# Memory-query products of the key/value gradients: from four 32-row products to one full product with a block diagonal operand

## The chip, the cores and the metric

The kernel runs on one core of a Trainium2 chip. The core has five engines with instruction streams of their own: TensorE (PE; its weight loads are listed as PEld), VectorE (DVE), ScalarE (ACT), GpSimd (POOL) and SyncE (SP), which in this kernel issues most of the DMA transfers. Sixteen DMA engines move the data between the chip's memory and the on-chip memory of 128 partitions. The metric is the device time of one execution in microseconds (us); lower is better.

## The reference

Forward and backward pass of a gated mix of two attention branches over 2048 tokens of width 576. Branch A has 32 query heads of width 18 and one shared key/value head. Branch B cuts the sequence into 64 segments of 32 tokens and carries 8 memory tokens from segment to segment; it has 32 heads of width 128. Cut to what matters:

```python
for s in range(n_seg):                       # 64 segments, in order
    h = concat([mem, x[s]])                  # 8 memory tokens, then 32 tokens
    q, k, v = h @ Wq, h @ Wk, h @ Wv         # 32 heads x 128
    p = softmax(mask(q @ k.T * scale))       # memory rows see the memory, tokens see memory and the past
    o = (p @ v) @ Wo
    mem = o[:8]                              # memory of the next segment
    outs.append(o[8:])
out = g * A(x) + (1 - g) * concat(outs)      # g = sigmoid(x . gate_w)
grads = vjp(grad_out)                        # x, all weights, mem0, gate_w
```

In the gradient, the key gradient of a token is the sum over the queries that saw it, `dk = dS^T q`, and its value gradient is `dv = P^T dO`. The queries are of two sorts: the tokens of the same segment, and the 8 memory rows of the segment. The change concerns the second sort. For 128 tokens (a tile of four segments) there are 4 x 8 = 32 memory queries per head.

## The kernel before

All of branch B's backward pass after the scores is in three stages, and the change touches the second and third of them, and a detail of the forward pass.

**Forward chain** (`b_chain_fwd`, woven with `a_pass1`): 64 segments in order. In each, the memory rows' attention ends with value products, 16 small matrix products into the tile `c_x`: eight with the weights `t2["v"]` on `PBm` (64 columns per region `u`), then eight with `vx` on `PBx` (32 columns), which add to them. `PBm` and `PBx` come from GpSimd (`expand`, line 264), one behind the other.

**Backward chain** (`b_chain_bwd`, woven with `a_pass2`): the segments in reverse order. Each segment is a list of 16 pieces (the `yield`s); after each piece the weaving emits one step of `a_pass2`, the backward pass of branch A: two products `b_S`, two `b_dP`, eight small ones into `b_acc`, one exponential on ScalarE (`b_E`) and two products on VectorE (`b_dS`). `a_pass2` loads `b_QS` from SP for every four steps; the load is emitted five steps before its first use and has three buffers.

From the fifth segment on, the pieces also carry key/value gradients of tokens that the chain has already passed: `kv_load`, `kv_mm` and `kv_out`, numbered by `n`. `n // 2` names a block of four heads `g` of a token tile `tt`; even `n` is the value gradient, odd `n` the key gradient. There are 4 x 8 x 11 / 2 = 176 of them (11 of the 16 token tiles), four per segment, in 44 segments. `kv_mm(n)` fills one bank of PSUM, the tile `r_x` of 128 tokens x 4 heads x 128:

- for each of the four heads, the memory queries: weights `kvS` (32 memory queries x 128 tokens, probabilities or score gradients), moving operand `kvR` (32 memory queries x 128, the rows of dO or of q), at the 32 partitions `rg` of the array;
- for each head, the tokens: weights `r_ks` (128 x 128), moving operand `r_kr` (128 x 128), which add to the same place.

`kv_mm(n)` ends with `kv_load(n + 2)`. For even `n` that is one load of `kvS` and two of `kvR` (dO from `mtok["dO"]`, q from `row_dram["q"]`), then `r_ks` and `r_kr`. `kvS` and `kvR` are one tile each, of which consecutive blocks use the four groups of 32 partitions in turn. All of these loads, those of the chain itself (`load_a`, `load_b`, `load_c`, `load_dT`) and those of `b_QS` stand in SP's one instruction stream, in the order in which the pieces emit them. In the built program each load from SP also waits for the eighth load before it to land.

**Behind the chain** (`b_post`): the remaining 6 token tiles, eight steps of four heads each, 48 steps. `st_KV` computes key and value gradients as above (tiles `y_pk`; operands `y_sB`, `y_mR` for the memory queries), `st_T` transposes them, `st_H` multiplies by the weights into `y_pdx`. `load_s` loads the memory queries of a whole token tile (twelve loads) a token tile ahead; `load` brings `y_ds`, `y_q`, `y_p`, `y_dO` and the transposed `y_dq` for every two steps.

Who writes the memory operands: `pq_dram` comes from GpSimd (`x_rows`, line 1009), with the memory index of the token tile in the order head-of-four `i`, memory row `q`, segment `s`; a segment's columns outside its own 32 tokens are zero.

Of the kernel before, what the change touches and what calls it, by code (L numbers as in the profile page):

```python
# [16 lines left out]
P = 128  # L17
# [5 lines left out]
E = 128  # L23
# [23 lines left out]
class Kern:  # L47
# [41 lines left out]
    def setup_consts(self, pool):  # L89
        nc = self.nc  # L90
        self.identB = pool.tile([P, P], BF16, name="identB")
        nc.gpsimd.memset(self.identB[:], 0.0)
        nc.gpsimd.affine_select(out=self.identB[:], in_=self.identB[:], compare_op=ALU.not_equal,
                                fill=1.0, base=0, pattern=[[-1, P]], channel_multiplier=1)
        self.identF = pool.tile([P, P], F32, name="identF")
        nc.vector.tensor_copy(self.identF[:], self.identB[:])

# [168 lines left out]

    def mem_rows(self, tt, c, cs):
        dO = self.mtok["dO"][tt * 32:(tt + 1) * 32, 1024 * c + cs.start:1024 * c + cs.stop]
        return (dO.rearrange("(s q) e -> q s e", s=4),
                self.row_dram["q"][4 * tt:4 * tt + 4, 32 * c:32 * c + 8, cs].rearrange("s q e -> q s e"))  # L270

# [57 lines left out]
    def b_chain_fwd(self, keep, sp, psum):  # L329
# [69 lines left out]
        for s in range(NSEG):  # L399
# [550 lines left out]
    def b_chain_bwd(self, wot, sp, kd, kvp, keep, psum):  # L950
# [7 lines left out]
        pads = {w: keep.tile([P, 8, 32], BF16, name=f"r_{w}pad") for w in ("p", "ds")}  # L958
        kvS = kvp.tile([P, 4, 2, P], BF16, name="r_kvS")
        kvR = kvp.tile([P, 2, 4, E], BF16, name="r_kvR")  # L960
        dT = kd.tile([P, 3, HB, 32], BF16, name="r_dT")
# [53 lines left out]
        def kv_at(n):  # L1015
            v, w = n // 2, n % 2
            return slice(32 * (v % 4), 32 * (v % 4) + 32), w, self.NTT - 1 - v // 8, v % 8

        def kv_load(n):
            if n >= NKV:  # L1020
                return
            rg, w, tt, g = kv_at(n)
            if w == 0:
                nc.sync.dma_start(kvS[rg].rearrange("p i x k -> p i (x k)"),
                                  self.pq_dram[tt, g // 2].rearrange("i q s h x k -> (q s) i h (x k)")[:, :, g % 2, :])
                for j, src in enumerate(self.mem_rows(tt, g // 2, slice(512 * (g % 2), 512 * (g % 2) + 512))):
                    nc.sync.dma_start(kvR[rg, j].rearrange("p i e -> p (i e)"), src)
            a = kvp.tile([P, 4, P], BF16, name="r_ks", bufs=3)
            nc.sync.dma_start(a[:], (self.dsx_dram if w else self.px_dram)[tt][:, 4 * g:4 * g + 4, :])
            b = kvp.tile([P, 4, P], BF16, name="r_kr", bufs=3)  # L1030
            nc.sync.dma_start(b[:].rearrange("p h e -> p (h e)"),
                              self.xtok["q" if w else "dO"][tt * P:(tt + 1) * P, 512 * g:512 * g + 512])
            kvl[n] = (a, b)

        def kv_mm(n):
            if not 0 <= n < NKV:
                return
            rg, w, tt, g = kv_at(n)
            a, b = kvl.pop(n)
            pk = psum.tile([P, 4, P], F32, name="r_x", bufs=1)  # L1040
            for i in range(4):
                self.mm(pk[:, i, :], lhsT=kvS[rg, i, w, :], rhs=kvR[rg, w, i, :], start=True, stop=False, tp=(rg.start, 0))
            for i in range(4):
                self.mm(pk[:, i, :], lhsT=a[:, i, :], rhs=b[:, i, :], start=False, stop=True)
            kvo[n] = pk
            kv_load(n + 2)

        def kv_out(n):
            if not 0 <= n < NKV:
                return  # L1050
            rg, w, tt, g = kv_at(n)
# [174 lines left out]
    def b_post(self, sp, rp, wH, psum):  # L1226
# [5 lines left out]
        NC = NG // 2  # L1232
        pdx, C, sB, mR, T_ = {}, {}, {}, {}, {}

        def load_s(n):
            tt = NTT - 1 - n
            if tt >= 0:
                sB[tt] = sp.tile([P, 4, 2, 2, P], BF16, name="y_sB", bufs=2)
                mR[tt] = sp.tile([P, 2, 8, E], BF16, name="y_mR", bufs=2)
                for c in range(4):  # L1240
                    r = slice(32 * c, 32 * c + 32)
                    nc.sync.dma_start(sB[tt][r].rearrange("p i h x k -> p i (h x k)"),
                                      self.pq_dram[tt, c].rearrange("i q s h x k -> (q s) i (h x k)"))
                    for j, src in enumerate(self.mem_rows(tt, c, slice(0, 1024))):
                        nc.sync.dma_start(mR[tt][r, j].rearrange("p u e -> p (u e)"), src)

# [15 lines left out]
        def st_KV(t):  # L1262
            tt, g, r, d = NTT - 1 - t // 8, t % 8, slice(4 * (t % 2), 4 * (t % 2) + 4), C[t // 2]
            pks = {w: psum.tile([P, 4, P], F32, name="y_pk", bufs=2) for w in ("dk", "dv")}
            c, h2 = slice(32 * (g // 2), 32 * (g // 2) + 32), g % 2
# [47 lines left out]
        load_s(0)  # L1313
        load(1, ("ds", "q", "p", "dO"))
        load(0, ("dq",))
        load(2, ("ds", "q", "p", "dO"))
        load(1, ("dq",))
        load(2, ("dq",))
        load_s(1)
# [837 lines left out]
```

## Time and profile before

| | |
|---|---|
| median of three runs | 5495.77 us (5483.73 to 5498.1) |
| profiled execution, from its first to its last instruction | 5509.8 us |
| mean granted clock of TensorE | 0.983 |
| DMA traffic | 1012.49 MB in 1107113 packets |

The profiled execution's own span is 14 us above the median; the profile gives no other time of it. Busy times of TensorE in the stages (windows of the profile):

| stretch, us | what runs | PE busy, us | DMA share |
|---|---|---|---|
| 420 to 2130 | forward chain with `a_pass1` | 1643.62 of 1710 | 0.62 |
| 2130 to 2815 | tokens' attention (`b_bulk`) | 612.16 of 685 | 0.81 |
| 2815 to 2954 | backward chain, before the first key/value gradient | 112.02 of 139 | 0.65 |
| 2954 to 4096 | backward chain with key/value gradients | 1096.18 of 1142 | 0.92 |
| 4096 to 4490 | backward chain, rest | 352.94 of 394 | 0.68 |
| 4490 to 4731 | `b_post` | 230.99 of 241 | 0.92 |
| 4731 to 5510 | weight gradients, last products | 757.31 of 779 | 0.66 |

How to read the lines that are shown below: a line of a tile names the line of the kernel, the engine, the operation, the tile written and the tiles read, how many there are, and the duration in ns (shortest/median/longest). Matrix products are all recorded at line 82, a helper, so they are told apart by their tiles. A timeline's line begins with its start and its duration in us; in square brackets stands how long the engine had been idle before it, and what released it. A matrix product's duration contains the way through the array, so the pace of products is read from the starts. "SPq" are the transfers that SP issues: the duration there is that of issuing, and is not counted as busy time of an engine; the DMA share is the mean busy share of the sixteen DMA engines.

### The profile page before, as it was taken

The page shows a single profiled execution, that of the slowest core. Times are in us where ns is not written, and L with a number is a line of the kernel's source. Part 1 is how long each engine was busy: PE and PEld are TensorE (multiplying, and loading weights), DVE is VectorE, ACT ScalarE, POOL GpSimd, SP SyncE. Part 2 cuts the span into 40 slices and gives each one's busy share as a digit, 9 for nine tenths or more (in the row PEclk, how much of TensorE's full clock was granted, in tenths as well). Part 3 has the DMA queues.
Part 4 walks back from the last instruction along what each step waited for, and adds up shares of the span by engine and source line. Part 5 has one row for each costly group of instructions (what it writes and reads, how often), then busy time and mean ns, then how long its engine had stood idle before and what let it go on. Part 6 is the DMA issues. An engine that isn't in the chain of part 4 may idle for free. (4 is left out here: it accounts for less than half of the span.)

```text
span 5509.8 us, 204884 instructions
## 1 busy us (share of the span) xinstructions
PE 5191.1 (94%) x87077; PEld 2903.4 (53%) x87077; DVE 3717.0 (67%) x6812; ACT 3494.6 (63%) x5264; POOL 2300.6 (42%) x4322
## 2 busy tenths in 40 slices
PE   7999999999999998999979999999998989999999
PEld 6434444444444445777744555555554457764444
DVE  5337888788888887888868888888888851121112
ACT  4327878788878886888858887778777752111101
POOL 4004555555555545555534444444444421122213
PEclk9999999999999998999989999999999999999999
DMA  6646666666665545888885899999987679976653
GB/s 215 229 173 135 136 136 135 134 137 140 138 133 121 117 108 163 256 253 261 253 257 153 206 216 205 201 206 211 204 189 145 141 167 274 262 222 228 208 161 122
DMA packets 1107113, 1012.49 MB, mean 184 GB/s; under 512 B 666674, under 2 KB 919355, under 8 KB 1096594
## 3 DMA queue, kind: packets, MB, share of 16 engines
q1 hardware_dynamic: 1002642, 752.11, 57.2%
q0 software_dynamic: 100016, 242.38, 14.3%
q8 instruction: 681, 11.16, 0.9%
q10 hardware_dynamic: 3536, 4.90, 0.3%
q14 instruction: 238, 1.95, 0.1%
HBM read 547.90 MB, written 383.13 MB: 169 GB/s over the span
## 5 line engine op out<-in xcount | busy, mean ns | idle before, releaser
L1736 DVE TENSOR_TENSOR a_W<-a_dP,a_E 128x512 bf16<-128x512 f32 x2048 | 1314.7, 684 | 276.2 <-issue 129.4
L1876 DVE TENSOR_TENSOR b_dS<-b_dP,b_E 128x512 bf16<-128x512 f32 x2048 | 1311.6, 684 | 245.4 <-issue 108.1
L1853 ACT ACTIVATE b_E<-b_S 128x1024 bf16<-128x1024 f32 x1024 | 1048.2, 1024 | 298.3 <-PE b_dP L82 229.8
L1706 ACT ACTIVATE a_E<-a_S 128x1024 bf16<-128x1024 f32 x1024 | 1049.9, 1025 | 261.2 <-PE a_dP L82 170.2
L82 PEld LDWEIGHTS <-b_QS 32*128 32x128 bf16 (+1 forms) x8192 | 257.5, 92 | 549.6 <-issue 481.1
L82 PE MATMUL r_pj<-WT,r_dT 128*32 128x288 bf16 x12288 | 496.0, 288 | 10.4 <-issue 10.2
L82 PE MATMUL b_S<-b_KV,b_QS 32*128 32x512 bf16 x2048 | 406.0, 387 | 97.5 <-ACT b_E L1853 62.4
L82 PE MATMUL w_acc<-w_d,w_h 128*128 128x512 bf16 (+1 forms) x2400 | 473.8, 379 | 0.0
L82 PE MATMUL a_S<-a_QD,l_KV 32*128 32x512 bf16 x2048 | 400.8, 385 | 41.8 <-ACT a_E L1706 35.3
L82 PE MATMUL b_acc<-b_dS,b_QS 128*32 128x512 bf16 x2048 | 427.8, 395 | 1.1 <-DVE b_dS L1876 0.9
L82 PE MATMUL a_acc<-a_W,l_WK 128*32 128x512 bf16 x4096 | 414.6, 391 | 0.3 <-DVE a_W L1736 0.2
L82 PE MATMUL a_acc<-a_E,l_VK 128*32 128x512 bf16 x4096 | 405.3, 381 | 10.2 <-issue 5.6
L82 PE MATMUL b_acc<-b_E,b_QS 128*32 128x512 bf16 x2048 | 410.2, 396 | 0.5 <-issue 0.5
L82 PE MATMUL b_dP<-b_KV,b_QS 32*128 32x512 bf16 x2048 | 404.7, 391 | 0.0
L82 PE MATMUL a_dP<-a_QD,l_KV 32*128 32x512 bf16 x2048 | 399.9, 387 | 0.0
L82 PEld LDWEIGHTS <-r_dT 128*32 128x32 bf16 x12288 | 333.3, 97 | 107.4 <-issue 16.8
L82 PEld LDWEIGHTS <-w_h 128*128 128x128 bf16 (+1 forms) x2688 | 229.9, 100 | 258.3 <-issue 6.6
L82 PEld LDWEIGHTS <-hm 128*32 128x32 bf16 x7680 | 204.0, 97 | 196.4 <-issue 2.6
L79 ACT CAST w_o<-w_acc 128x512 bf16<-128x512 f32 x54 | 31.6, 585 | 384.3 <-PE w_acc L82 367.9
L783 POOL TENSOR_TENSOR x_P<-x_E,x_r 128x512 bf16<-128x512 bf16 x128 | 152.7, 1193 | 293.6 <-DVE x_r L780 293.6
L77 DVE CAST w_o<-w_acc 128x512 bf16<-128x512 f32 x54 | 37.3, 691 | 335.2 <-PE w_acc L82 308.9
L82 PEld LDWEIGHTS <-l_KV 32*128 32x128 bf16 x4096 | 121.7, 91 | 254.3 <-issue 209.6
(464 smaller groups left out, 10903.3 us busy)
## 6 DMA issues: line engine op xcount, KB each, us to landing
b_QS<-qs_dram SPq DMA_DIRECT2D x256, 256.0 KB
dOx_dram<-p_tok SPq DMA_DIRECT2D x16, 1024.0 KB
c_vx<-vx_dram SPq DMA_DIRECT2D x64, 256.0 KB
krow_dram<-c_k POOLq DMA_DIRECT2D x64, 256.0 KB
qrow_dram<-c_q POOLq DMA_DIRECT2D x64, 256.0 KB
vrow_dram<-c_v POOLq DMA_DIRECT2D x64, 256.0 KB
x_q<-qx_dram SPq DMA_DIRECT2D x32, 512.0 KB
x_k<-kx_dram SPq DMA_DIRECT2D x32, 512.0 KB
```

Of the source, the lines that this page charges most:

```text
L77: nc.vector.tensor_copy(out, in_)
L79: nc.scalar.copy(out, in_)
L82: return self.nc.tensor.matmul(out, lhsT, rhs, start=start, stop=stop, tile_position=tp, skip_group_check=True)
L783: nc.gpsimd.tensor_tensor(out=o[:, r, :], in0=Et[:, :, lo:lo + n], in1=rl[:].unsqueeze(2).to_broadcast([P, 4, n]), op=ALU.mult)
L1706: nc.scalar.activation(E_[n][:], S.pop(n)[:], ACT.Exp, scale=SCALEA)
L1736: nc.vector.tensor_tensor(out=W_[n][:, i, :], in0=dP[i][:], in1=E_[n][:, i, :], op=ALU.mult)
L1853: nc.scalar.activation(E_[n][:], S.pop(n)[:], ACT.Exp, scale=SCALEA)
L1876: nc.vector.tensor_tensor(out=D_[n][:, i, :], in0=dP[i][:], in1=E_[n][:, i, :], op=ALU.mult)
```

## The change

- The memory queries of four heads become one operand. `kvS` is now a tile of 128 rows (4 heads x 32 memory queries), and `kvR` a tile of 128 rows x (dO or q) x 4 heads x 128 in which only the blocks of a row's own head are filled: a block diagonal. The other blocks are zeroed once by VectorE when the tiles are made, and never written again. One product of 128 rows and 512 columns replaces four of 32 rows and 128 columns.
- `kv_mem` makes the tiles, two pairs in the chain and four in `b_post`, and clears them. `kv_mem_load` loads one block of four heads: S in one load, R in eight, one for each head and for dO and q, each of 32 rows of 256 bytes.
- In `b_post`, `load_s` loads by step (`t + 4`), not by token tile, and `st_KV` finishes one of the two tiles before it begins the other.
- In the forward chain the two loops over `u` become one: for each region the product on `PBm` is followed by that on `PBx`.
- `identF`, a copy of the identity matrix for branch A's forward pass, is made where it is used.

In the built program, TensorE's 704 short products into `r_x` become 176 and the 384 into `y_pk` become 96; SP issues 528 loads more in the chain and 360 more in `b_post`; the order of everything else stays.

```diff
+    def kv_mem(self, pool, name, bufs):
+        S = [pool.tile([P, 2, P], BF16, name=f"{name}S{i}") for i in range(bufs)]
+        R = [pool.tile([P, 2, 4, E], BF16, name=f"{name}R{i}") for i in range(bufs)]
+        for t in R:
+            self.nc.vector.memset(t[:].rearrange("p x i e -> p (x i e)").bitcast(F32), 0.0)
+        return S, R
+
+    def kv_mem_load(self, S, R, tt, g):
+        c, h = g // 2, g % 2
+        self.nc.sync.dma_start(S[:].rearrange("p x k -> p (x k)"),
+                               self.pq_dram[tt, c].rearrange("i q s h x k -> (i q s) h (x k)")[:, h, :])
+        for i in range(4):
+            r, c0 = slice(32 * i, 32 * i + 32), 512 * h + 128 * i
+            for x, src in enumerate((
+                    self.mtok["dO"][tt * 32:(tt + 1) * 32, 1024 * c + c0:1024 * c + c0 + E].rearrange("(s q) e -> q s e", s=4),
+                    self.row_dram["q"][4 * tt:4 * tt + 4, 32 * c:32 * c + 8, c0:c0 + E].rearrange("s q e -> q s e"))):
+                self.nc.sync.dma_start(R[r, x, i, :], src)
...
                 self.mm(po[:, u, :], lhsT=t2["v"][:, u, :], rhs=PBm[:, u, :], start=True, stop=False)
-            for u in range(8):
                 self.mm(po[:, u, 0:32], lhsT=vx[:, u, :], rhs=PBx[:, u].rearrange("p c q -> p (c q)"),
...
-                nc.sync.dma_start(kvS[rg].rearrange("p i x k -> p i (x k)"),
-                                  self.pq_dram[tt, g // 2].rearrange("i q s h x k -> (q s) i h (x k)")[:, :, g % 2, :])
-                for j, src in enumerate(self.mem_rows(tt, g // 2, slice(512 * (g % 2), 512 * (g % 2) + 512))):
-                    nc.sync.dma_start(kvR[rg, j].rearrange("p i e -> p (i e)"), src)
+                self.kv_mem_load(kvS[g % 2], kvR[g % 2], tt, g)
...
-            for i in range(4):
-                self.mm(pk[:, i, :], lhsT=kvS[rg, i, w, :], rhs=kvR[rg, w, i, :], start=True, stop=False, tp=(rg.start, 0))
+            self.mm(pk[:].rearrange("p i e -> p (i e)"), lhsT=kvS[g % 2][:, w, :],
+                    rhs=kvR[g % 2][:, w].rearrange("p i e -> p (i e)"), start=True, stop=False)
...
-                for c in range(4):
-                    r = slice(32 * c, 32 * c + 32)
-                    nc.sync.dma_start(sB[tt][r].rearrange("p i h x k -> p i (h x k)"),
-                                      self.pq_dram[tt, c].rearrange("i q s h x k -> (q s) i (h x k)"))
-                    for j, src in enumerate(self.mem_rows(tt, c, slice(0, 1024))):
-                        nc.sync.dma_start(mR[tt][r, j].rearrange("p u e -> p (u e)"), src)
+        sB, mR = self.kv_mem(sp, "y_m", 4)
+
+        def load_s(t):
+            if t < NG:
+                self.kv_mem_load(sB[t % 4], mR[t % 4], NTT - 1 - t // 8, t % 8)
...
-            for x, w in ((1, "dk"), (0, "dv")):
-                for i in range(4):
-                    self.mm(pks[w][:, i, :], lhsT=sB[tt][c, i, h2, x, :], rhs=mR[tt][c, x, 4 * h2 + i, :],
-                            start=True, stop=False, tp=(c.start, 0))
-            for w, s_, r_ in (("dk", "ds", "q"), ("dv", "p", "dO")):
+            for x, w, s_, r_ in ((1, "dk", "ds", "q"), (0, "dv", "p", "dO")):
                 pk = pks[w]
+                self.mm(pk[:].rearrange("p i e -> p (i e)"), lhsT=sB[t % 4][:, x, :],
+                        rhs=mR[t % 4][:, x].rearrange("p i e -> p (i e)"), start=True, stop=False)
...
-                    if t % 8 == 7:
-                        load_s(t // 8 + 2)
+                    load_s(t + 4)
...
+        self.identF = keep.tile([P, P], F32, name="identF")
+        nc.vector.tensor_copy(self.identF[:], self.identB[:])
```

More of the change, by code (lines that the diff above doesn't have):

```diff
@@ L94, in setup_consts @@
                                 fill=1.0, base=0, pattern=[[-1, P]], channel_multiplier=1)
-        self.identF = pool.tile([P, P], F32, name="identF")
-        nc.vector.tensor_copy(self.identF[:], self.identB[:])
     XT0 = 5
@@ L265, in expand @@
                                      in1=self.bmask[:].unsqueeze(1).to_broadcast([P, n, 4, 8]), op=ALU.mult)
[L267 to L270, printed above, removed]
+    def kv_mem(self, pool, name, bufs):
[14 more added lines that the diff above has]
+                self.nc.sync.dma_start(R[r, x, i, :], src)
     def m_rows(self, t, c):
@@ L958, in b_chain_bwd @@
         pads = {w: keep.tile([P, 8, 32], BF16, name=f"r_{w}pad") for w in ("p", "ds")}
-        kvS = kvp.tile([P, 4, 2, P], BF16, name="r_kvS")
-        kvR = kvp.tile([P, 2, 4, E], BF16, name="r_kvR")
+        kvS, kvR = self.kv_mem(kvp, "r_kv", 2)
         dT = kd.tile([P, 3, HB, 32], BF16, name="r_dT")
@@ L1016, in kv_at @@
             v, w = n // 2, n % 2
-            return slice(32 * (v % 4), 32 * (v % 4) + 32), w, self.NTT - 1 - v // 8, v % 8
+            return w, self.NTT - 1 - v // 8, v % 8
         def kv_load(n):
@@ L1037, in kv_mm @@
                 return
-            rg, w, tt, g = kv_at(n)
+            w, tt, g = kv_at(n)
             a, b = kvl.pop(n)
             pk = psum.tile([P, 4, P], F32, name="r_x", bufs=1)
-            for i in range(4):
-                self.mm(pk[:, i, :], lhsT=kvS[rg, i, w, :], rhs=kvR[rg, w, i, :], start=True, stop=False, tp=(rg.start, 0))
+            self.mm(pk[:].rearrange("p i e -> p (i e)"), lhsT=kvS[g % 2][:, w, :],
+                    rhs=kvR[g % 2][:, w].rearrange("p i e -> p (i e)"), start=True, stop=False)
             for i in range(4):
@@ L1050, in kv_out @@
                 return
-            rg, w, tt, g = kv_at(n)
+            w, tt, g = kv_at(n)
             o = kvp.tile([P, 4, P], BF16, name="r_kvo", bufs=2)
@@ L1232, in b_post @@
         NC = NG // 2
[L1233 to L1239, printed above, removed]
-                for c in range(4):
-                    r = slice(32 * c, 32 * c + 32)
-                    nc.sync.dma_start(sB[tt][r].rearrange("p i h x k -> p i (h x k)"),
-                                      self.pq_dram[tt, c].rearrange("i q s h x k -> (q s) i (h x k)"))
-                    for j, src in enumerate(self.mem_rows(tt, c, slice(0, 1024))):
-                        nc.sync.dma_start(mR[tt][r, j].rearrange("p u e -> p (u e)"), src)
+        pdx, C, T_ = {}, {}, {}
+        sB, mR = self.kv_mem(sp, "y_m", 4)
+        def load_s(t):
+            if t < NG:
+                self.kv_mem_load(sB[t % 4], mR[t % 4], NTT - 1 - t // 8, t % 8)
         def load(c, names):
@@ L1314, in b_post @@
         load(1, ("ds", "q", "p", "dO"))
+        load_s(1)
         load(0, ("dq",))
         load(2, ("ds", "q", "p", "dO"))
+        load_s(2)
         load(1, ("dq",))
+        load_s(3)
         load(2, ("dq",))
-        load_s(1)
         hist = [self.hist_to_dram(a, b, sp, psum, "y_pt", 2, g)
```

3 lines of the change are left out of this document (1 added, 2 removed).

## The prediction

> **What bounds the kernel now.** I read the views in this order: the windows of the two stages in which the change works, the instructions of the tiles that it replaces, SP's timeline (SP issues these loads), and TensorE's timeline and waits beside it. The windows first; the columns are the stretch, its length, busy time (and instructions) of PE, PEld, DVE, ACT and POOL, the granted clock, the share of the DMA engines and GB/s.
>
> ```profile
> core 0: us, PE busy (x) PEld busy (x) DVE busy (x) ACT busy (x) POOL busy (x), PEclk, DMA share, GB/s
> 2954.00:4096.00 1142.00, 1096.18 (x22992) 591.54 (x22989) 956.28 (x1659) 920.96 (x1224) 550.39 (x1008) 0.99 0.92 205
> 4490.00:4731.00 241.00, 230.99 (x2488) 185.73 (x2487) 41.73 (x116) 55.95 (x105) 33.86 (x61) 0.96 0.92 247
> ```
>
> The first is the part of the backward chain that carries key/value products: 176 of them, four per segment, so 44 segments at 1142/44 = 25.95 us. The second is the stage behind the chain (`b_post`). TensorE is busy 96% of both, and nearly all its gaps are filled, so it sets the pace; but the DMA engines stand at 0.92, and nothing here shows SP, whose issues are not counted as busy. So I took the replaced tiles:
>
> ```profile
> L82 PE MATMUL r_x<-r_kvR,r_kvS x704: 211/214/309, 2954.0 to 4095.7; 32*128 32x128 bf16 x176
> L1024 SPq DMA_DIRECT2D r_kvS<-pq_dram x88: 325/424/1334, 2935.6 to 4073.9; - x88
> L1027 SPq DMA_DIRECT2D r_kvR<-dOm_dram x88: 671/692/1170, 2936.0 to 4074.3; - x88
> L1027 SPq DMA_DIRECT2D r_kvR<-qrow_dram x88: 643/644/2316, 2936.8 to 4075.1; - x88
> L82 PE MATMUL y_pk<-y_mR,y_sB x384: 214/214/309, 4499.7 to 4720.3; 32*128 32x128 bf16 x192
> L1245 SPq DMA_DIRECT2D y_mR<-dOm_dram x24: 660/661/727, 4492.8 to 4663.2; - x24
> L1245 SPq DMA_DIRECT2D y_mR<-qrow_dram x24: 643/644/709, 4493.6 to 4663.9; - x24
> ```
>
> The reader is to see the price of issuing one load of 32 memory rows: 0.64 to 0.69 us, the same whether a row's piece is 1 KB (`r_kvR`) or 2 KB (`y_mR`). It isn't the bytes that are paid for. SP issues one behind the other:
>
> ```profile
> 3515.44 0.34 SPq L1834 DMA_DIRECT2D b_QS<-qs_dram  x1
> ...
> 3519.27 0.53 SPq L1834 DMA_DIRECT2D b_QS<-qs_dram  x1
> 3519.85 0.42 SPq L1024 DMA_DIRECT2D r_kvS<-pq_dram  x1
> 3520.32 0.69 SPq L1027 DMA_DIRECT2D r_kvR<-dOm_dram  x1
> 3521.05 0.64 SPq L1027 DMA_DIRECT2D r_kvR<-qrow_dram  x1
> ```
>
> About 0.05 us lies between an issue and the next. I summed SP's rows of its timeline from 3200 to 3800 us: 665 issues in 23 segments, 475.0 us. With the gaps that is 475.0 + 665 x 0.05 = 508 us of 600, or 20.65 + 1.45 = 22.1 us of issuing in a segment of 26.1 us. SP is 85% full. And it is already late at times, at a load that has nothing to do with the memory queries:
>
> ```profile
> 3518.63 0.39 PE L82 MATMUL r_x<-WoTt,dm 128*32 128x512 bf16 x4
> 3520.38 0.39 PE L82 MATMUL b_S<-b_KV,b_QS 32*128 32x512 bf16 x2 [1.36 <-DMA b_QS<-qs_dram]
> ...
> 3524.38 0.39 PE L82 MATMUL r_x<-r_kvR,r_kvS 32*128 32x128 bf16 x4
> 3524.71 0.40 PE L82 MATMUL r_x<-r_kr,r_ks 128*128 128x128 bf16 x4
> 3525.04 0.39 PE L82 MATMUL b_S<-b_KV,b_QS 32*128 32x512 bf16 x2
> ```
>
> `b_QS` was issued at 3515.44 and used from 3520.38: landing takes some 5 us. The code issues it five steps of 1.55 us, 7.75 us, before its use, so SP may be no more than about 2.7 us behind the order of the program before TensorE waits.
>
> **The change, part by part.**
>
> *Wide products.* From 3524.38 to 3524.71 four products of 128 columns take 0.33 us. One of 512 columns goes at the pace of the weight gradients, 420.3 us for 1920, 0.22 us. Saved: 0.11 x 176 = 19 us in the chain. In `b_post` eight short ones per step (31.2 us for 384, 0.65 us) become two (0.44 us): 0.21 x 48 steps = 10 us. These 29 us count only where TensorE sets the pace; in the sum below it doesn't, so they count nothing.
>
> *Loads in the chain.* Per block of four heads there was one load of S and two of R. Now it is one of S and eight of R, each with 32 pieces of 256 B from the same pattern of rows. S keeps its bytes and its 128 pieces, and I leave it at 0.47. The trace has no such R load. The nearest rows are the two `r_kvR` lines, which differ only in the length of a piece, which didn't matter between 1 and 2 KB: I take their median, 0.66. The cheapest row with pieces of 256 B for 32 partitions (with four pieces per partition) is
>
> ```profile
> L683 SPq DMA_DIRECT2D x_kmB<-km_dram x128: 302/430/1392, 2133.0 to 2785.8; - x128
> ```
>
> whose 0.30 I keep as the lower end. Per segment (two blocks): 16 x (0.66 + 0.05) = 11.4 us come, 2 x (0.69 + 0.68 + 0.10) = 2.9 us go (means of that stretch). SP's work becomes 22.1 + 8.5 = 30.6 us in a segment that TensorE could do in 25. SP becomes the pace: 30.6 - 25.95 = 4.6 us x 44 = **+204 us**, rounded to +200.
> The other ends: SP's rows hold stalls. At their shortest durations they make 18.2 us with gaps; if the stalls vanish, 18.2 + 8.5 = 26.7, +33 us. Upwards: in the built program each load from SP waits for the eighth before it to land, and at 3535.24 an `r_kvR` load waited for an `r_k` load issued 6.3 us earlier. At 6.3/8 = 0.78 us per load, 41 loads (29 + 12) take 32 us; +6.3 x 44 = 277 us. What waits behind the R loads on SP are `r_ks`/`r_kr` of the same product, then the loads of the next segment's chain, and `b_QS`; TensorE waits for `b_QS` first, in front of `b_S`, and with it the exponentials of ScalarE and the products of VectorE.
>
> *Loads in b_post.* Each of 48 steps now issues its own 9 loads; before, 12 served eight steps. Two steps: 2 x (0.44 + 8 x 0.655) + 18 x 0.05 = 12.3 us; with four loads of `y_ds`, `y_q`, `y_p`, `y_dO` and a transposed `y_dq`, at least 1.92 + 1.32 us, 15.5 us; at their means there (2.37 + 0.20 + 1.77) 16.6 us. So 24 x 15.5 = 372 to 398 us, where TensorE needs about 216. TensorE can't run ahead: the product of step t wants its own loads. I take 385. The first R load waits for VectorE to clear the buffers, behind a copy that ends at 4496.9, while SP arrives at 4492.8: +4.5 us. Last product at 4490 + 4.5 + 385 + 2 (landing) = 4881 for 4720: **+160 us** (145 to 190; at 0.30 + 0.05 per load two steps are 9.9 us, 238 us in all, +15).
>
> *Value products in the forward chain.* Eight products on `c_PBm` stood ahead of the first on `c_PBx`; now one does. POOL's and TensorE's rows:
>
> ```profile
> 1005.45 0.63 POOL L264 TENSOR_TENSOR c_PBx<-c_pn,bmask 128x256 bf16<-128x256 bf16 x1
> ```
>
> ```profile
> 1005.95 0.41 PE L82 MATMUL c_x<-c_PBm,c_v 128*128 128x64 bf16 x8
> 1006.19 0.36 PE L82 MATMUL c_x<-c_PBx,c_vx 128*128 128x32 bf16 x8
> 1006.73 0.39 PE L82 MATMUL a_S<-a_QD,l_KV 32*128 32x512 bf16 x2 [0.18 <-ACT a_E L1706]
> ```
>
> `c_PBx` is done at 1006.08; the second product would now be ready at 1005.98, so it waits some 0.1 us. The 0.24 us of the eight covered that. The same step then waits 0.18 us for ScalarE anyway, which takes the delay in. 64 segments: 0 to 10 us; I take +3.
>
> *Small things.* The clearing of R on VectorE (two and four tiles): a clear of twice that size took 912 ns (`x_kmB`), so 0.5 us each, beside other work but for the 4.5 us above. `identF` moves one copy of 0.5 us: nothing. Matrices of 1 and 2 KB per partition change place in memory: nothing.
>
> Sum against the profiled execution: 5509.8 + 200 + 160 + 3 = 5873. It stands 14 us above the median of the runs; **5860 us** against 5495.77.
>
> **Two rules beside the rows.** The issues in the timeline cost 0.64 us and more for 8 to 64 KB, and that sets my sum. The Trainium skill, "DMA: Bandwidth & Descriptors", section Issuing engines are not separate DMA queues, holds that the sequencer's time to start a DMA is usually small beside the DMA. By that rule the added loads would stay hidden; this trace disagrees, with SP 85% full.
> A second rule speaks against the change in another way. The Trainium skill, "DMA: Bandwidth & Descriptors", section Specifications, states that transfers under 512 B fall below line rate because the engine reads, modifies and writes. No row here separates such pieces; what it would do is rival 4.
>
> **The rivals.**
> 1. *The loads hide, the products win* (faster). Issuing would cost by bytes, and a load of 8 KB a quarter of one of 32 KB: 0.17. Then SP has 22.1 + 16 x 0.22 - 2.9 = 22.7 us per segment, and in `b_post` two steps take 2 x (0.49 + 8 x 0.22) = 4.5 us and 3.2 to 4.3 for the rest, under the 9.0 that TensorE needs (216/24). The 29 us are gained: 5496 - 29 = 5467. The chain is hidden below 0.37 per R load, `b_post` below about 0.25. Against it: 0.64 for 32 KB and for 64 KB alike.
> 2. *SP keeps its pace in the chain only.* The stalls go, 26.7 us per segment: 5496 + 33 + 160 = 5690. For it: the added loads are small and DMA traffic per time falls. Against it: R's loads come in bursts of 6 us, and `b_QS` bears 2.7.
> 3. *Cheap issue*, 0.30: the chain is hidden and gains up to 19, `b_post` loses 15: 5495. Same objection as for 1.
> 4. *The 16 DMA engines become the bound.* The window 3200 to 3800 has 0.94 of them busy and 166642 packets of SP's queue in 81.5% of 16 x 600 us, 47 ns each. So they work 0.94 x 26.1 = 24.5 us per segment. R's pieces go from 128 of 1 KB to 512 of 256 B: 384 x 47 ns / 16 = 1.1 us more, 25.6, below SP's 30.6. If one of 256 B took four times 47 ns they would reach 30 us, SP's own; at eight times 512 x 376 / 16 = 12 us, 36 us per segment, +440 and with `b_post` 6100. For it: 0.94 is near full. Against it: 112970 of that window's 178576 packets are under 512 B already, and the mean is 47 ns.
>
> **How the numbers follow.** Forecast 0.79, its own range 5740 to 5990 (chain +100, with half of SP's stalls gone, to +277; `b_post` +145 to +190, and 25 more for landings that the fuller queue delays). Rival 2: 0.08. Rival 4, or loads that land later still: 0.07. Rival 1: 0.03. Rival 3: 0.03. The range of eight in ten is 5670 to 6010: it takes in rival 2 and 20 us on either side, and leaves out the others. Runs differ by 0.26%, so under 0.3% (16 us) is no change. Faster 0.03, within 0.3% 0.03, slower 0.94.
>
> **What would show it.** SP's timeline of the chain without gaps, 41 loads per segment, R loads at 0.64 to 0.69 us; segments of about 30.6 us; waits of `b_S` for `b_QS` of some 5 us per segment, where now they sum to 9.8 us in 1142; `b_post` near 400 us with TensorE busy little more than half and `y_pk` waiting for `y_mR`. The forward part unchanged within 10 us. I am wrong if an R load's row reads 0.35 us or less, or if segments stay at 26 us although it reads 0.66, which would mean that SP had more room than I counted.

## The result, and the profile after

The changed kernel takes 5904.61 us (median of five runs, 5899.32 to 5934.0) against 5495.77 us (5483.73 to 5501.76): 1.0756 times as long, 95% interval 1.0736 to 1.0776. It is slower, and 45 us above the forecast of 5860, inside the range of 5670 to 6010.

The profiled executions have spans of 5509.8 and 5932.3 us, 422.5 apart. The profile of the kernel after is of the longest of its five executions, so its stages add up to 13 us more than the medians' 409. By the starts of the products that mark the stages:

| stage | before, us | after, us | difference |
|---|---|---|---|
| start to the first `b_S` (forward chain, `b_bulk`) | 2812.98 | 2814.25 | +1.3 |
| first to last key/value product of the chain, 44 segments | 1141.5 | 1380.3 | +238.8 |
| the same per segment | 25.94 | 31.37 | +5.43 |
| `b_post`, from the end of the chain to the first weight gradient | 241.9 | 419.8 | +178 |
| weight gradients to the end | 779.2 | 783.0 | +3.9 |

The two stages of the prediction hold the loss, and the forward part none of it that these profiles show: in the other kernels below, the first `b_S` comes between 2802 and 2823 us. The windows of the kernel after (columns as in the prediction):

```profile
2956.00:4336.00 1380.00, 1149.81 (x22456) 577.86 (x22454) 960.43 (x1658) 922.96 (x1224) 549.68 (x1005) 0.89 0.73 170
4730.00:5149.00 419.00, 272.11 (x2218) 200.90 (x2210) 45.69 (x119) 58.73 (x105) 34.07 (x62) 0.81 0.53 141
```

TensorE fell from 96% busy to 83% and 65%, and the DMA engines from 0.92 to 0.73 and 0.53. No engine of the page is full. The tiles of the kernel after (shortest/median/longest duration in ns):

```profile
L281 SPq DMA_DIRECT2D r_kvR<-dOm_dram x352: 643/644/2527, 2937.8 to 4319.2; - x176
L281 SPq DMA_DIRECT2D r_kvR<-qrow_dram x352: 643/644/2121, 2938.6 to 4319.9; - x176
L82 PE MATMUL r_x<-r_kvR,r_kvS x176: 389/390/609, 2955.8 to 4336.1; 128*128 128x512 bf16 x176
L281 SPq DMA_DIRECT2D y_mR<-dOm_dram x192: 643/644/1859, 4738.2 to 5134.4; - x192
```

A load of 8 KB costs SP as much as one of 32 KB did. So SP issues R loads without a pause, and `b_QS` comes late behind them; SP's timeline, then TensorE's for `b_S` (in brackets the idle time before it):

```profile
3595.04 0.64 SPq L281 DMA_DIRECT2D r_kvR<-qrow_dram  x1
3595.73 1.26 SPq L281 DMA_DIRECT2D r_kvR<-dOm_dram  x1
3597.03 0.64 SPq L281 DMA_DIRECT2D r_kvR<-qrow_dram  x1
...
3598.74 1.30 SPq L1000 DMA_TRANSPOSE r_dT<-dqx_dram  x1
3600.14 0.52 SPq L1833 DMA_DIRECT2D b_QS<-qs_dram  x1
```

```profile
3595.61 0.39 PE L82 MATMUL b_S<-b_KV,b_QS 32*128 32x512 bf16 x2
3597.44 0.39 PE L82 MATMUL b_S<-b_KV,b_QS 32*128 32x512 bf16 x2 [0.46 <-ACT b_E L1852]
3604.95 0.61 PE L82 MATMUL b_S<-b_KV,b_QS 32*128 32x512 bf16 x2 [5.92 <-DMA b_QS<-qs_dram]
3606.79 0.61 PE L82 MATMUL b_S<-b_KV,b_QS 32*128 32x512 bf16 x2
```

TensorE's waits, with total us, times, longest: for `b_QS` in the chain's window, before the change and after it; for `y_mR` in that of `b_post`; then SP's own at the start of `b_post`:

```profile
PE b_S L82 <- DMA b_QS<-qs_dram: 9.8, 10, 2.0
```

```profile
PE b_S L82 <- DMA b_QS<-qs_dram: 197.7, 63, 6.5
```

```profile
PE y_pk L82 <- DMA y_mR<-qrow_dram: 134.2, 36, 9.1
```

```profile
SPq L281 <- DVE y_mR L269: 5.7, 1, 5.7
```

The wait for `b_QS` is now 4.5 us in each segment, which is most of the 5.43 that a segment became longer.

### The profile page after: what moved, and what is told of

Its sections match the earlier page's. It is cut to its first block, busy times and chain, and to the rows that moved or that the text cites. A ratio compares the mean times of both kernels' runs of the same rounds, so it can differ in the third digit from the quotient of the medians.

```text
span 5932.3 us, 204293 instructions
## 1 busy us (share of the span) xinstructions
PE 5287.7 (89%) x86080; PEld 2911.9 (49%) x86261; DVE 3725.7 (63%) x6818; ACT 3506.2 (59%) x5264; POOL 2300.3 (39%) x4322
## 5 line engine op out<-in xcount | busy, mean ns | idle before, releaser
L82 PE MATMUL b_S<-b_KV,b_QS 32*128 32x512 bf16 x2048 | 429.6, 410 | 287.9 <-DMA b_QS<-qs_dram 215.4
L82 PE MATMUL b_acc<-b_dS,b_QS 128*32 128x512 bf16 x2048 | 448.7, 419 | 1.7 <-DVE b_dS L1875 0.9
L82 PE MATMUL b_acc<-b_E,b_QS 128*32 128x512 bf16 x2048 | 432.6, 419 | 0.0
L82 PE MATMUL a_S<-a_QD,l_KV 32*128 32x512 bf16 x2048 | 401.8, 386 | 30.6 <-ACT a_E L1705 24.5
L82 PE MATMUL b_dP<-b_KV,b_QS 32*128 32x512 bf16 x2048 | 428.2, 414 | 0.0
```

Of the source, the lines that this page charges most:

```text
L82: return self.nc.tensor.matmul(out, lhsT, rhs, start=start, stop=stop, tile_position=tp, skip_group_check=True)
```

## The experiments

The theory: SP's one stream bounds both stages, and the R loads fill it. The rivals: the DMA engines suffer under pieces of 256 bytes; the wide product itself is slow; the lower clock sets the time; the bursts, not the sum, make `b_QS` late. The table has the measured times, the segment and `b_post` (defined as above). Each ratio is to the kernel before as it ran beside that kernel on the same chip, where it took 5496 to 5519 us. In the two kernels marked * the profile lacks the record of one wide product in each segment, the chain's last among them; there the segment is taken from the first to the last product of the tokens, which by that count is 25.96 us before the change.

| kernel | time, us | ratio to before (95%) | segment, us | `b_post`, us |
|---|---|---|---|---|
| before | 5495.77 | | 25.94 | 241.9 |
| after | 5904.61 | 1.0756 (1.0736 to 1.0776) | 31.37 | 419.8 |
| loads cut, products short | 5980.18 | 1.0873 (1.0853 to 1.0893) | 31.44 | 468.5 |
| no R loads | 5506.73 | 1.0008 (0.9994 to 1.0022) | 25.41 | 257.1 |
| R on GpSimd | 5814.0 | 1.0580 (1.0562 to 1.0598) | 30.86 | 329.8 |
| `b_QS` earlier | 5897.47 | 1.0724 (1.0708 to 1.0740) | 30.63 | 426.4 |
| expanded on the chip | 5496.89 | 0.9968 (0.9956 to 0.9980) | 25.69 | 234.6 |
| half of R | 5662.43 | 1.0273 (1.0252 to 1.0294) | 27.61 | 310.1 |
| half of R, `b_QS` earlier | 5608.62 | 1.0172 (1.0148 to 1.0195) | 26.62* | 315.1 |
| R off SP, later | 5770.02 | 1.0471 (1.0448 to 1.0493) | 31.16 | 275.4 |
| ... one half earlier | 5779.73 | 1.0465 (1.0427 to 1.0504) | 30.97 | 278.0 |
| ... the other half too | 5726.98 | 1.0395 (1.0351 to 1.0438) | 29.76 | 279.1 |
| R of one row | 5756.19 | 1.0429 (1.0398 to 1.0461) | 29.43 | 331.4 |
| expanded, `b_QS` earlier | 5482.69 | 0.9940 (0.9920 to 0.9960) | 25.74* | 232.6 |

**Loads cut, products short.** The kernel before, with its four products of 32 rows, but each R load cut by head.

```diff
-                for j, src in enumerate(self.mem_rows(tt, g // 2, slice(512 * (g % 2), 512 * (g % 2) + 512))):
-                    nc.sync.dma_start(kvR[rg, j].rearrange("p i e -> p (i e)"), src)
+                for i in range(4):
+                    c0 = 512 * (g % 2) + E * i
+                    for j, src in enumerate(self.mem_rows(tt, g // 2, slice(c0, c0 + E))):
+                        nc.sync.dma_start(kvR[rg, j, i, :], src)
```

> The kernel before, with its short products, but with the memory rows loaded head by head: per block of four heads one S load and eight R loads of 32 pieces of 256 B (chain), per token tile 4 S and 64 R loads (b_post; the changed kernel has 8 and 64). If SP's issuing sets the pace: chain near the 31.4 us per segment of the changed kernel (before 25.95), b_post near 400 us, 5880 to 5910 in all; the short products are hidden. If the wide products or the new tiles were the cause: about 5500.

5980.18 us. The segment, 31.44, is that of the changed kernel without its wide product, so the loads alone make the chain's loss. `b_post` missed the expectation, and the time with it: there I issued the 64 R loads of a token tile in one burst, ahead of the steps' own loads, and TensorE waited 133.8 us, in four waits, for `y_q`, which stands behind such bursts.

**No R loads.** The changed kernel without R loads after the first blocks.

```diff
-        for i in range(4):
+        for i in range(4 if first else 0):
```

> The changed kernel without R loads after the first two blocks of the chain and the first four of b_post (leaves out the memory rows of dO and q of all later blocks). If SP's issuing sets the pace: SP has 22.1 - 2.9 = 19 us of issuing per segment, TensorE sets the pace again, and the wide products show their gain: chain 25.2 to 25.6 us per segment, 5450 to 5490 in all. If anything else of the change costs the time (the wide products, a lower granted clock by itself): above 5600.

5506.73 us, no difference from before. The segment is as expected, the time 17 us above the upper end of what I had expected. The window of its chain:

```profile
2948.00:4066.00 1118.00, 1076.43 (x22457) 578.49 (x22455) 955.75 (x1658) 919.21 (x1224) 549.75 (x1005) 1.00 0.89 205
```

Everything slow about the change hangs on the R loads, whichever way. What is left of a gain is 23 us in the chain (1141.5 to 1118.2), TensorE being the bound again at 96%; `b_post` gave back 15 us, because the first four steps' 32 R loads stand at its start.

**R on GpSimd.** One word of the changed kernel.

```diff
-                self.nc.sync.dma_start(R[r, x, i, :], src)
+                self.nc.gpsimd.dma_start(R[r, x, i, :], src)
```

> The changed kernel, its R loads issued by GpSimd instead of SP: same loads, same pieces, same DMA engines. If SP's issuing sets the pace: SP has 19 us per segment, GpSimd 12.5 + 16 x 0.58 = 21.8 of 26, so the chain is near 26 us; in b_post GpSimd issues 8 x 0.58 = 4.6 us per step where TensorE needs 4.5, some 40 us more than before: 5520 to 5600 in all. If the small pieces on the DMA engines, or their landing, set the pace: as the changed kernel, 5850 to 5910.

5814.0 us, neither case: less than a quarter of the loss went. GpSimd's timeline, and VectorE's beside it:

```profile
3607.77 0.60 POOL L281 DMA_DIRECT2D r_kvR<-dOm_dram  x1
3608.30 0.61 POOL L281 DMA_DIRECT2D r_kvR<-qrow_dram  x1
3608.83 0.32 POOL L1003 COPY r_dspad<-r_dS 128x64 bf16<-128x64 bf16 x1
```

```profile
3609.18 0.45 DVE L1007 STREAM_TRANSPOSE r_dsq<-r_dspad 128x256 bf16<-128x256 bf16 x1 [5.32 <-POOL r_dspad L1003]
```

Eight loads of 0.57 us now stand ahead of a small copy on which the chain depends. VectorE waits for it 184.5 us in all, and TensorE behind VectorE (159.2 us before `b_dP`). The trouble moved from one queue to another.

**`b_QS` earlier.** The loads of `b_QS` four steps earlier, with a fourth buffer; to make room, `r_kr` has two buffers and a mask lies in a pool that is closed early.

```diff
-                QS = sp.tile([P, 2, 512], BF16, name="b_QS", bufs=3)
+                QS = sp.tile([P, 2, 512], BF16, name="b_QS", bufs=4)
...
-                    load(n // 4 + 2)
+                    load(n // 4 + 3)
```

> The changed kernel with b_QS loaded four steps (6.2 us) earlier, in four buffers; r_kr has two buffers instead of three for the space, and a tile of constants is made in a pool that is closed. If SP is full (in the profile of the changed kernel 26.7 us of issuing and 2.5 us of gaps per segment of 31.4): the segment can't fall below 29.2 us, the waits move to other loads, 5810 to 5905. If SP has room and only the bursts of R loads make b_QS late: the segment goes back to about 26 us, 5660 to 5700.

5897.47 us. TensorE's waits in its chain:

```profile
PE r_x L82 <- DMA r_kr<-qx_dram: 74.0, 38, 3.3
PE b_dP L82 <- DVE b_dS L1876: 57.2, 35, 3.4
PE r_x L82 <- DMA r_kr<-dOx_dram: 31.6, 29, 2.3
...
PE b_S L82 <- DMA b_QS<-qs_dram: 8.8, 12, 2.2
```

The wait for `b_QS` went from 197.7 to 8.8 us, and others took its place. SP's rows from 3300 to 3900 us sum to 526.5 us of issuing and 46.6 of short gaps: a load that has been made early only hands the wait to the next load in a stream that is full. That the next one is `r_kr` may be due in part to the buffer that it lost in this edit; in the last run below, with the same two buffers and SP's list as short as before, the waits for `r_kr` are 6.2 us. The granted clock rose from 0.89 to 0.94 and the segment shrank by 0.7 us only, so the clock doesn't set the time either.

**Expanded on the chip.** R is loaded as before the change (two loads per block), and four copies of 32 x 256 per block put it on the diagonal: GpSimd in the chain, VectorE in `b_post`. The wide product stays.

```diff
+    def kv_expand(self, eng, R, src):
+        for i in range(4):
+            eng.tensor_copy(R[32 * i:32 * i + 32, :, i, :], src[:, :, i, :])
```

> The wide products with the loads of before: the R rows are loaded into one compact tile (chain: 2 loads per block; b_post: 8 per token tile, S in 4), and the block diagonal is made on the chip by four copies of 32 x 256 per block, on GpSimd in the chain and on VectorE in b_post. If SP's issuing was the whole loss: SP as before (22 us of 26), GpSimd +3 us per segment; chain 25.3 to 26.0, b_post 225 to 240: 5465 to 5500. If the copies come late for their product (they wait on GpSimd behind a load's issue and the old product): 5500 to 5560.

5496.89 us where the kernel before took 5516.9 on the same chip: 0.3% faster, as expected. The copies took 0.39 us each on GpSimd and 0.22 on VectorE, beside other work. So the wide product is worth having: the chain is 11 us shorter and `b_post` 7, of the 29 that the prediction had counted for TensorE alone. It is the way of making the operand that cost 400 us.

**Half of R.** Only dO's R loads; those of q are left out after the first blocks.

```diff
-                self.nc.sync.dma_start(R[r, x, i, :], src)
+                if first or x == 0:
+                    self.nc.sync.dma_start(R[r, x, i, :], src)
```

> The changed kernel with the four R loads of dO per block, and without the four of q after the first blocks (leaves out the memory rows of q of later blocks). If SP's issuing sets the pace with a knee: SP 19.2 + 8 x 0.71 = 24.9 us per segment, chain near 26 us; b_post 2 x (0.49 + 4 x 0.70) + 3.2 to 4.3 = 9.8 to 10.9 us per two steps instead of 9.0, +20 to +45: 5500 to 5570. If each load costs its share wherever SP stands: half way, about 5690.

5662.43 us, nearer to the second case. The chain has no free room for eight loads: the segment rises by 2.2 us with the first eight R loads and by 3.8 with the second. TensorE waited for `b_QS` 72.5 us here. SP's rows from 3300 to 3900 us sum to 486.5 us of issuing, 44.4 of short gaps and 69.1 of waits: with a ninth of its time in waits, SP already delays TensorE. By what ended them, SP's waits (some lie inside the issuing) are 72.6 us for TensorE to be done with a tile and 41.1 for an earlier load to land; the second sort is the subject of the run with one row.

**Half of R, `b_QS` earlier.** Both edits at once.

> The kernel with half of the R loads, and b_QS four steps earlier as in the run before (r_kr in two buffers). SP issues 24.5 us of a segment of 27.6 there. If the bursts ahead of b_QS cost the rest: chain 25.3 to 26.0 us per segment, about 5580 in all. If SP is as good as full at 24.5 of 27.6: 27.0 to 27.6, 5640 to 5665.

5608.62 us, between the two expectations. With half of the loads the earlier `b_QS` is worth 1.0 us a segment (with all of them 0.7): at that load bursts matter, but the 26.62 us are still 1.2 above the kernel without R loads, with 43.6 us of waits left in 600 of SP. What is left is a wait for `r_kr` (54.2 us, 1.2 a segment). A full stream would make it, and so would the buffer that `r_kr` lost; the runs don't separate the two.

**R off SP, later.** All R loads off SP: in the chain GpSimd issues them behind its critical work, in `b_post` GpSimd takes those of dO and ScalarE those of q.

```diff
             x_rows(s, 1, dS[:, 0, :])
+            kv_load_R(n0 + 2)
...
             load_dT(s - 1, 1)
+            kv_load_R(n0 + 4)
```

> All R loads as in the changed kernel, none of them on SP: in the chain GpSimd issues them, emitted behind its work for the running segment (not ahead of the copy for which VectorE waits, as in the first try on GpSimd); in b_post GpSimd issues those of dO, ScalarE those of q. If SP's issuing was the loss: chain 25.4 to 26.2 us per segment, b_post 235 to 260 us, 5460 to 5540 in all. If the small pieces on the DMA engines or their landing were: 5750 or more.

5770.02 us, a miss. `b_post` came down to 275.4, but the chain stood at 31.16 us a segment with SP's stream nearly half empty. TensorE's waits there:

```profile
PE r_x L82 <- DMA r_kvR<-dOm_dram: 159.4, 42, 7.3
```

So R itself was late, 3.8 us in each wait. I took it to be the loads at the segment's end and moved those into GpSimd's longest idle stretch:

> As the run with all R loads off SP (GpSimd in the chain, GpSimd and ScalarE in b_post), with one edit: the eight R loads of every second block are issued three pieces earlier, in the stretch of about 7 us in which GpSimd's timeline of that run stands idle (3598.5 to 3605.2), instead of at the segment's end, behind the store of dxr, where the next segment's first wide product then waited for them 159 us in all (42 waits, about 3.8 us in each segment). Theory that SP's issuing alone made the changed kernel slow: with SP's list short and the R rows on the chip in time, the chain runs as it does without R loads, 25.4 to 26.2 us a segment; b_post stays at its 275 us; the time is 5520 to 5580. Rival, that the 704 and 384 small loads cost something beyond the queue that issues them (the DMA engines, or their landing late wherever they are issued): the segment stays at 28 us or more and the time at 5640 or above; 5580 to 5640 would say that both have a share.

5779.73 us, no change: I had moved the wrong half. The expectation's account of where the wait stands is wrong too. TensorE's timeline of this run:

```profile
3623.66 0.39 PE L82 MATMUL r_x<-r_kvR,r_kvS 128*128 128x512 bf16 x1
3631.18 0.38 PE L82 MATMUL r_x<-r_kvR,r_kvS 128*128 128x512 bf16 x1 [2.79 <-DMA r_kvR<-dOm_dram]
```

The waiting product is the segment's second block's, whose loads GpSimd issues from 3621.64 to 3627.6. Next, those went earlier as well:

```diff
                     x_rows(s, 0, pT[:, 0, :])
+                    kv_load_R(n0 + 2, (0, 1))
...
+            kv_load_R(n0 + 2, (2, 3))
             for c in range(4):
```

> The last two runs left the R loads of a segment's second block where GpSimd issues them from 3621.6 to 3627.6, and that block's first wide product at 3631.2 waited for the last of them to land (3.8 us in each segment in both runs; not the first block's loads, which the last run moved earlier). Here those eight loads go earlier too: four behind the store of the score gradient's rows (GpSimd's timeline had 2.35 us idle there), four behind the product r_prod (2.4 us idle). Theory that only queues and places matter (SP's issuing in the changed kernel, GpSimd's place in these runs): TensorE waits for R in the chain no more, the segment falls to 25.5 to 27 us and the time to 5545 to 5610. Rival, that the small loads cost something wherever they are issued: taking the wait away frees at most its 3.8 us and something else waits instead, the segment stays at 27.2 us or more and the time at 5620 or above.

5726.98 us. TensorE's waits in the chain, and GpSimd's timeline:

```profile
PE r_pj L82 <- POOL r_hx L1212: 70.2, 38, 5.1
PE r_x L82 <- POOL r_dSB L262: 41.1, 42, 3.2
```

```profile
3612.59 0.54 POOL L284 DMA_DIRECT2D r_kvR<-dOm_dram  x1 [0.23 <-DMA dTm_dram<-r_dTc]
3615.26 0.54 POOL L284 DMA_DIRECT2D r_kvR<-qrow_dram  x1 [2.13 <-DMA r_kvR<-dOm_dram]
3615.80 0.57 POOL L1068 DMA_DIRECT2D dvx_dram<-r_kvo  x1
3616.36 0.23 POOL L1212 COPY r_hx<-r_hs 64x32 bf16<-64x32 bf16 x1
```

The wait for R is gone (under 1 us of it is left), as the first theory said; the time is what the rival said, because something else waits: a load that itself waits for an earlier load to land holds up the copy `r_hx`, and the chain with it. In each of the four placements on GpSimd its order of work holds something up, R itself or a copy behind it, so they don't show what the loads cost the DMA engines.

**R of one row.** That was the question of the last run. All R loads stay on SP at their places, but bring only the first of their 32 rows.

```diff
-                self.nc.sync.dma_start(R[r, x, i, :], src)
+                if first:
+                    self.nc.sync.dma_start(R[r, x, i, :], src)
+                else:
+                    self.nc.sync.dma_start(R[32 * i:32 * i + 1, x, i, :], src[0, 0:1, :])
```

> The changed kernel with every R load kept on SP at its place, but cut, after the first blocks of the chain and the first four steps of b_post, to the first of its 32 rows: 256 bytes instead of 8 KB; the other rows keep old values. SP issues the same number of loads as in the changed kernel, and the DMA engines have nearly nothing of them to move. What costs SP 0.64 to 0.70 us a load isn't known: if it is the instruction, a row costs as much, and by the theory that SP's issuing bounds the stages the segment stays at 31 us, b_post at 400 to 420 and the time at 5880 to 5910, which the theory that the DMA engines are the bound would not allow. If it is the rows, the tile line shows 0.25 to 0.40 us a load; then SP's list falls by 16 x 0.3 to 0.45 us to some 20 to 22 us a segment plus its waits, the segment to 25.5 to 27 and the time to 5520 to 5600, which both theories allow, and the issue time per row is what the run measures.

5756.19 us: neither case. The issue became cheap, and the stage stayed slow. The tile's lines, the window of the chain, and TensorE's wait in it:

```profile
L284 SPq DMA_DIRECT2D r_kvR<-dOm_dram x344: 211/240/1947, 2964.4 to 4229.0; - x172
L284 SPq DMA_DIRECT2D r_kvR<-qrow_dram x344: 211/233/1552, 2965.1 to 4229.2; - x172
```

```profile
2953.00:4248.00 1295.00, 1128.62 (x22460) 574.20 (x22459) 959.40 (x1658) 922.74 (x1224) 549.53 (x1005) 0.92 0.77 177
```

```profile
PE b_S L82 <- DMA b_QS<-qs_dram: 137.7, 45, 5.0
```

From 3300 to 3900 us SP's rows sum to 422.5 us of issuing, 44.9 of short gaps and 132.6 of waits; per segment 20.7, 2.2 and 6.5 us. That is hardly more issuing than before the change (20.4 and 1.7, from the same window). The waits grew, from 3.7 us per segment to 6.5, and are of another sort: before, most were for TensorE to be done with a tile. SP's own in this run, and its timeline:

```profile
SPq L284 <- DMA r_dT<-dvx_dram: 26.0, 20, 3.5
SPq L991 <- PE b_dP L82: 23.6, 13, 3.2
SPq L284 <- DMA b_QS<-qs_dram: 20.1, 31, 1.7
```

```profile
3605.94 1.80 SPq L1003 DMA_TRANSPOSE r_dT<-dvx_dram  x1
3607.83 1.18 SPq L996 DMA_DIRECT2D r_dx<-dmx_dram  x1
3609.11 0.37 SPq L998 DMA_DIRECT2D r_q<-qrow_dram  x1
3610.04 0.32 SPq L274 DMA_DIRECT2D r_kvS<-pq_dram  x1
3610.45 0.41 SPq L284 DMA_DIRECT2D r_kvR<-dOm_dram  x1
3610.91 0.23 SPq L284 DMA_DIRECT2D r_kvR<-qrow_dram  x1
3611.70 0.21 SPq L284 DMA_DIRECT2D r_kvR<-dOm_dram  x1
3612.88 0.21 SPq L284 DMA_DIRECT2D r_kvR<-qrow_dram  x1
3616.22 0.21 SPq L284 DMA_DIRECT2D r_kvR<-dOm_dram  x1
```

The load at 3616.22 is the eighth behind the transposed load at 3605.94 and stands 3.1 us until that has landed; all that is queued behind it, `b_QS` too, stands with it. Waits of R loads and others for an earlier load to land sum to 100.3 us in this window, 4.9 per segment; before the change they were 30.6, 1.3 per segment. So an added load costs a place among eight even if its issue is short and it brings only 256 bytes. A segment of 41 loads took 29.43 us, 0.72 us a load; in the changed kernel it is 31.37/41 = 0.77.

This also ends the DMA engines as the rival for most of the loss: with 256 bytes instead of 8 KB per load, and a share of 0.77, two thirds of the chain's loss (3.5 of 5.4 us a segment) are still there. The last third went with the bytes and with the issue time together; this run doesn't separate them.

**Expanded, `b_QS` earlier.** The expanding kernel with the `b_QS` edit, and the forward chain's two loops as before the change.

> The block diagonal made on the chip, with b_QS four steps earlier (four buffers, r_kr in two), and the two loops of value products of the kernel before. If the waits for b_QS (14.5 us in the chain with key/value products, 15 us in the rest of the backward chain) go and nothing takes their place: ratio to before 0.990 to 0.994. If SP now waits for r_kr's two buffers: 0.996 or more.

5482.69 us where the kernel before took 5513.14 on that chip: 0.6% faster, and the fastest of all. In its profile the chain with key/value products is 9.3 us shorter than before and `b_post` 9.3; the stretch from the first `b_S` to the first key/value product is 7 us shorter (133.8 us for 141.0), and the earlier `b_QS` gains nothing in the chain beyond the 11 of the expanding kernel.

## Why the prediction was right, and where it wasn't

- *Direction and place*: right. SP's stream bounds both stages; wait for `b_QS` 4.5 us per segment (5 forecast), 41 loads per segment, `b_post` 419.8 us (near 400), TensorE 65% busy there and waiting for `y_mR`.
- *"Loads in the chain", +200*: measured +239, under-sized, within its ends of +33 and +277. The forecast was 22.1 + 8.5 = 30.6 us of issuing and no waits. From 3300 to 3900 us the kernel after has 511.6 us of issuing, 48.2 of gaps and 40.3 of waits in 19.1 segments: 26.7 + 2.5 + 2.1 = 31.4. Three sizes were off and two cancel. R loads took 0.70 us with 0.06 between issues, not 0.66 and 0.05: 16 of them 12.2 us, +0.8. The old loads lost 2.2 us of stalls, and 2.1 us of waits came.
- *"Loads in b_post", +160*: measured +178, inside 145 to 190. SP arrived at the buffers 5.7 us ahead of VectorE's clearing (4.5 forecast), and 548 issues from 4736 to 5134 us took 348.4 us, with 27.2 of gaps and 20.6 of waits; the forecast had no waits.
- *"Value products in the forward chain", +3*: the stage ends 1.3 us later; since its end lies between 2802 and 2823 us in the other profiles, a term of 3 us is not shown either way.
- *The wide products "count nothing"*: right for the changed kernel. Their 29 us show where the loads don't stand in the way: 18 in the expanding kernel, 23 in the chain without R loads.
- *Rival 2, SP keeps its pace in the chain* (26.7 us): the stalls in the old loads did shrink, but the R loads took 0.76 us with their gap and not 0.71, and waits came; 31.37.
- *Rival 3, cheap issue*: its price was wrong in kind. It gave 5495 us if an R load cost 0.30; with a median of 0.24 the kernel took 5756. I had reckoned SP as a sum of issue times, and taken the wait for the eighth load only as an upper end. It is a second bound beside the first: make the issue cheap, and the places bind. In the changed kernel the trace speaks for the issuing: with its gaps it makes 29.2 us of the 31.4, and SP's waits for an earlier load to land are 28.1 us in the 600, 1.5 a segment, where before the change they were 1.3. No run gives SP more places, so the second bound is read from the timeline and not tested.
- *Rival 1 and the rule on issuing* (the Trainium skill, "DMA: Bandwidth & Descriptors", section Issuing engines are not separate DMA queues: the time to start a DMA is usually small beside the DMA): for a single load the trace fits it, 0.64 us of issuing beside the 4.8 us from the issue of `b_QS` at 3600.14 to its use. What fails is rival 1's conclusion that the loads stay hidden: 41 issues a segment fill one stream, and 400 us are lost. The prediction's 0.64 us "for 8 to 64 KB" had loads of 32 and 64 KB behind it; the 8 KB are measured in the kernel after. The same section says that all issuers share the 16 DMA engines; no run here tests that, since what held up the runs on GpSimd was the order of its work.
- *Rival 4, the DMA engines*: not the bound, since two thirds of the chain's loss stay with one-row loads, as above.

## What to carry to other kernels

Count a queue's DMAs before their bytes: where a queue's stream is 85% full, cutting a load into four costs, as long as the issue doesn't go by bytes, four times its issue and four of the places in flight, and the wait falls on the load that comes late behind them (`b_QS` here), not on the data that were cut. Loads that are moved to another in-order queue delay that queue's small copies; look for what the chain needs behind each place. Here a block diagonal operand was cheaper spread by copies on an engine with idle time than by loads.

## What the hardware showed that I had not expected

- The issue time of these loads did not go by their bytes: 32 memory rows took 0.64 us for 256 B, 1 KB and 2 KB each, one row 0.21 us at the shortest and 0.24 at the median. The number of rows alone isn't the rule either: S, with 128 rows of 512 B, took 0.42. What else sets it the runs don't show.
- TensorE gets a lower clock after a wait. After the wait of 5.92 us shown above, `b_S` takes 0.61 us where it had taken 0.39, and goes on so at 3608.97. In the chain of that kernel no wait up to 3.77 us did this, and every one from 4.85 us on; between them some did. In the run with one row a wait of 2.78 us did it already, and one of 4.67 didn't. The trace's own record of the granted clock has only 1.0 and 0.5, in stretches of whole multiples of 3.41 us on one fixed grid, so it seems to count how a wait lies on that grid, not its length alone. The clock of 0.89 and 0.81 in the two stages goes with the waits: without the R loads it was 1.00 in the chain; with the waits for `b_QS` gone it was 0.94, and the segment hardly shorter. The Trainium skill, "TensorE: Matmul & The Clock Gate", section Part 1: The HAM clock gate (the "warmup" mystery), has the clock halved after an idle window of about 3.4 us; the record of the clock agrees with the half and with the 3.41 us.
- A stage can have no full engine, a DMA share of 0.73 and a lower clock, and still be bound: by one instruction stream that no row of the page's busy times shows.
